# Values of two heads and sums of four heads side by side on TensorE, and the first batch taken in by units

## The chip, the cores and the metric

The kernel runs on one core of one Trainium2 chip. The metric is the device time of one execution in microseconds (us). TensorE (PE in the profile) multiplies matrices into PSUM; VectorE (DVE), ScalarE (ACT) and GpSimd (POOL) work on what lies in SBUF and PSUM; transfers are issued by queues of SyncE (SP), ScalarE and GpSimd. "PEld" is TensorE's loading of the stationary operand of a matmul.

## The reference

Causal attention with a window of 64 positions, followed by a gated two-layer network whose weights are shared by all 4608 tokens.

```python
# q, k, v: (batch 8, heads 8, positions 576, 64) float32
scores = q @ k.T / sqrt(64)                 # per batch and head
mask   = (0 <= row - col) & (row - col < 64)
attn   = softmax(where(mask, scores, -1e9))
x      = (attn @ v) as (8 * 576, 8 * 64)    # heads side by side: 4608 x 512
gate   = maximum(x @ w_gate, 0)             # 512 x 1536
out    = (gate * (x @ w_val)) @ w_out       # 1536 x 512; out is 4608 x 512 float32
```

## The kernel before

The 4608 rows are cut into 24 units of 192 rows (three units to a batch, 8 heads each), and two units make a tile of 384 rows. Attention of a unit gives x turned (features on partitions) in `xt`; the network then runs per tile: `hidden` (groups h of the profile) and `output` (groups op). A small scheduler, the Weaver `W`, places the instructions of the attention units between those of the network: `W.at(t, fn)` queues a piece at a time t of its own clock, and `plan_unit` does so for all the pieces of one unit. Each engine then runs its instructions in the order in which they were written.

In a unit the scores come turned as well: the 128 keys that 64 queries can see lie on partitions. The exponentials `p` are multiplied by a band mask on VectorE (units 0 and 1 add a bias on TensorE before the exponential instead). Values and the sums for the softmax come out of one matmul: each head's value tile holds 64 columns of values and 64 columns of ones.

```python
v16s = [persist.tile([128, UB, H, 128], FP16) ...]     # UB = 3 windows, per head 64 values | 64 ones

def v_load(u):                                          # upper half of each window from memory
    for w in range(UB):
        nc.gpsimd.dma_start(v16s[uu][64:128, w, :, 0:64], v[b, :, k0:k0 + 64] ...)
def v_low(u):                                           # lower half: copy of the window before
    ...                                                 # one or two nc.vector.tensor_copy

def u_pv_wide(u):                                       # units 2 to 23
    d["pv"] = [a_ps.tile([128, 2, 2, 256], FP32, tag="a") for _ in range(2)]
    for c in (0, 2, 1, 3):
        for e in range(2):
            h = 2 * c + e
            for w in range(UB):
                nc.tensor.matmul(d["pv"][c % 2][:, c // 2, e, 64 * w:64 * w + 64],
                                 v16[:, w, 128 * h - 64 * e:128 * h - 64 * e + 128],   # 128 columns
                                 d["p"][h % G][:, h // G, 64 * w:64 * w + 64], ...)

def u_copy(u, n):   # two ScalarE copies for each n in 0, 1: values of even and of odd heads
    ...
def u_sum(u, half): # two VectorE turns for each half: sums of even and of odd heads
    for e in range(2):
        nc.vector.transpose(to[64 * e:64 * e + 64, half::2],
                            d["pv"][half][64 - 64 * e:128 - 64 * e, :, e, 0:U])
def u_back(u):      # reciprocal of one column of each turned block, turned back
    nc.vector.reciprocal(d["rT"], d["sT"]...[:, :, 0:1])
    nc.vector.transpose(d["rs"], d["rT"].to_broadcast([128, nb, 32]))
def u_norm(u):      # xt = values * rs
    nc.vector.tensor_tensor(xt_tile(u // 2)[:, :, c0:c0 + U], d["xs"], rs, MUL)
```

Units 0 and 1 use a narrow form of it, `u_pv`: values of two heads on the two halves of the output's partitions (64 stationary columns each), and then sums from a tile `ones` of 64 columns, in the same way.

q and k of a batch are loaded whole, and turned by VectorE in blocks of 32 (`qk_trans`). The first batch:

```python
for hh in range(2):
    k_first(hh)                    # k in float32 by SyncE's queue, rounded by ScalarE
for hh in range(2):
    qk_load(0, "q", hh)            # q by GpSimd's queue, in float16
...
W.at(7.0, lambda: qk_trans(0, "q", 0)) ; W.at(9.9, lambda: qk_trans(0, "q", 1)) ; ...
W.at(5.3, lambda: u_bias(0)) ; W.at(5.4, lambda: heat(11, ...))   # heat: matmuls of zeros
W.at(6.4, lambda: w_load(*G3[0], 13.7)) ; ...          # nine weight parts of 512 KB
W.at(21.0, lambda: v_ones(2, nc.vector)) ; W.at(21.0, lambda: v_ones(0, nc.vector))
plan_unit(2, 23.0, ...) ; plan_unit(3, 42.15, ...) ; plan_unit(4, 49.3) ; plan_unit(5, 56.95, ...)
T = 67.0                           # then two units to each tile, T += 25.805
...
W.advance(13.7)
ready(1); hidden(0, 0, U, 0, 4, 4)           # first half of tile 0, first third of the features
ready(2); hidden(0, U, TT, 0, 4, 4)          # second half
hidden(0, 0, TT, 4, NF, 4); output_by_rows(0)
ready(3); hidden(1, 0, U); output(1, (0,))
ready(4); hidden(1, U, TT); output(1, (1, 2))
for t in range(2, NU // 2): ...              # whole tiles
```

Of the kernel before, what the change touches and what calls it, by code (L numbers as in the profile page):

```python
# [42 lines left out]
def kernel(  # L43
# [43 lines left out]
    v16s = [persist.tile([128, UB, H, 128], FP16, name=f"v16_{i}") for i in range(UB)]  # L87
# [4 lines left out]
    ident = consts.tile([128, 128], FP16)  # L92

# [21 lines left out]
    def v_ones(i, eng):  # L115
        eng.memset(v16s[i][64 if i == 0 else 0:, 0, :, 64:128], 1.0)
        for w in range(1, UB):
            eng.memset(v16s[i][:, w, :, 64:128], 1.0)  # L118

    def k_zeros():  # L120
        nc.vector.memset(kTs[1][:, :, 0:64], 0.0)

    def constants():
        nc.vector.memset(kTs[0][:, :, 0:64], 0.0)
        nc.vector.memset(v16s[0][0:64, 0], 0.0)
        nc.vector.memset(ones, 1.0)
        nc.vector.memset(ones0, 1.0)
        nc.vector.memset(ones0[0:64], 0.0)

# [40 lines left out]
    def k_first(hh):  # L170

        k32 = nat["k32", hh] = x_sb.tile([128, S // 32 * D], FP32, name="k32", bufs=2)
        nc.sync.dma_start(k32, k[0, G * hh:G * hh + G].rearrange("h (i j) d -> (h i) (j d)", i=32))

    def k_round(hh, part, parts):
        n = S // 32 * D // parts
        if part == 0:
            nat[0, "k", hh] = a_in.tile([128, S // 32 * D], FP16, name=f"k{hh}", bufs=2)
        nc.scalar.copy(nat[0, "k", hh][:, n * part:n * part + n], nat["k32", hh][:, n * part:n * part + n])  # L179
# [8 lines left out]
    def v_load(u):  # L188
        b, uu = divmod(u, UB)
        for w in range(UB):  # L190
            k0 = U * uu + 64 * w
            nc.gpsimd.dma_start(v16s[uu][64:128, w, :, 0:64], v[b, :, k0:k0 + 64].rearrange("h p d -> p h d"))  # L192

    def v_low(u):

        uu = u % UB
        if uu > 0:
            nc.vector.tensor_copy(v16s[uu][0:64, 0, :, 0:64], v16s[uu - 1][64:128, UB - 1, :, 0:64])
        nc.vector.tensor_copy(v16s[uu][0:64, 1:UB, :, 0:64], v16s[uu][64:128, 0:UB - 1, :, 0:64])

    def u_bias(u, gs=range(G)):

        d = units.setdefault(u, {})
        if "st" not in d:
            st_tiles(u)
        d["biased"] = True
        for to in d["st"][0] + d["st"][1] if u == 0 else [d["st"][0][g] for g in gs]:
            n = 1 if u == 0 else 2
            nc.tensor.matmul(to[:, 0:n * U].rearrange("p (n c) -> p n c", c=64), ident,
                             bias[:, None, :].to_broadcast([128, n * UB, 64]),  # L210
                             start=True, stop=False, skip_group_check=True)
# [6 lines left out]
    def st_tiles(u):  # L218
        d = units.setdefault(u, {})
        one = lambda name: f_ps.tile([128, 512], FP32, name=name, tag="h")  # L220
        two = lambda name: a_ps.tile([128, 2, 512], FP32, name=name, tag="a")
        if u == 0:
            d["st"] = [[one("st") for _ in range(G)]]
            halves = [two("st") for _ in range(2)]
            d["st"].append([halves[g // 2][:, g % 2] for g in range(G)])
        elif u == 1:
            half = two("st")
            d["st"] = [[half[:, 0], half[:, 1], one("st"), one("st")]] * 2
        else:
            halves = [two("st") for _ in range(2)]  # L230
            d["st"] = [[halves[g // 2][:, g % 2] for g in range(G)]] * 2
        if u == 0:
            d["spare"] = d["st"][1][3][:, 256:512]
            d["st"] = [[x[:, 0:512 if hh == 1 and g == 3 else 256] for g, x in enumerate(row)] for hh, row in enumerate(d["st"])]

    def u_st(u, hhs=(0, 1)):
        d = units.setdefault(u, {})
        kT, qT = kTs[(u // UB) % 2], qTs[(u // UB) % 2]
        biased = "biased" in d
        if not biased:  # L240
            st_tiles(u)
        ks = U * (u % UB)
        for hh in hhs:
            for w in range(UB):
                c = U * (hh if u else 0) + 64 * w
                for dh in range(2):
                    for g in range(G):
                        rows = slice(32 * g, 32 * g + 32)
                        nc.tensor.matmul(  # L249
                            d["st"][hh][g][:, c:c + 64],  # L250
                            kT[rows, hh, ks + 64 * w:ks + 64 * w + 128, dh],
                            qT[rows, hh, ks + 64 * w:ks + 64 * w + 64, dh],
                            start=(dh == 0 and not biased), stop=(dh == 1),
                            skip_group_check=biased)
        d.setdefault("p", [None] * G)
        return 0.49

    def u_exp(u, g, hh=None):
        d = units[u]
        if not hh:  # L260
            d["p"][g] = a_p.tile([128, 2, U], FP16, name="p")
        if hh is None:
            nc.scalar.activation(d["p"][g].rearrange("p h c -> p (h c)"), d["st"][0][g][:, 0:2 * U], ACT.Exp, scale=scale)  # L263
        else:
            nc.scalar.activation(d["p"][g][:, hh], d["st"][hh][g][:, 0:U], ACT.Exp, scale=scale)
# [6 lines left out]
    def u_pv(u, cs=(0, 2, 1, 3)):  # L272
# [3 lines left out]
        v16 = v16s[u % UB]  # L276
        if u == 0 and cs[0] == 0:
            d["pv"] = [f_ps.tile([128, 2, U], FP32, name="pv", tag="h") for c in cs]
        elif u == 0:
            both = a_ps.tile([128, 2, 512], FP32, name="pv", tag="a")  # L280
            d["pv"] += [both[:, n, 0:2 * U].rearrange("p (s c) -> p s c", s=2) for n in range(2)]
        else:
            halves = [a_ps.tile([128, 2, 512], FP32, name="pv", tag="a") for _ in range(2)]
            d["pv"] = [halves[c % 2][:, c // 2, 0:2 * U].rearrange("p (s c) -> p s c", s=2) for c in range(NC)]
        for c in cs:
            for w in range(UB):
                for e in range(2):
# [3 lines left out]
                        v16[:, w, h, 0:64], d["p"][h % G][:, h // G, 64 * w:64 * w + 64],  # L291
                        start=(w == 0), stop=True, skip_group_check=True)
            for w0, w1, one in ((0, 1, ones0), (1, UB, ones)) if u % UB == 0 else ((0, UB, ones),):
                for e in range(2):
                    h = 2 * c + e
                    nc.tensor.matmul(
                        d["pv"][c][64 * e:64 * e + 64, 1, 64 * w0:64 * w1],
                        one, d["p"][h % G][:, h // G, 64 * w0:64 * w1],
# [3 lines left out]
    def u_pv_wide(u):  # L302

        d = units[u]
        v16 = v16s[u % UB].rearrange("p w h d -> p w (h d)")
        d["pv"] = [a_ps.tile([128, 2, 2, 256], FP32, name="pv", tag="a") for _ in range(2)]
        for c in (0, 2, 1, 3):
            for e in range(2):
                h = 2 * c + e
                for w in range(UB):  # L310
                    nc.tensor.matmul(  # L311
                        d["pv"][c % 2][:, c // 2, e, 64 * w:64 * w + 64],
                        v16[:, w, 128 * h - 64 * e:128 * h - 64 * e + 128],
                        d["p"][h % G][:, h // G, 64 * w:64 * w + 64],
                        start=(e == 0 and w == 0), stop=True,
                        skip_group_check=True)
        return 0.7

    def u_copy(u, n):
# [3 lines left out]
        if u < 2:  # L323
            c = n if u == 0 else (0, 2, 1, 3)[n]
            nc.scalar.copy(d["xs"][:, c], d["pv"][c][:, 0])
        else:
            for e in range(2):
                rows = slice(64 * e, 64 * e + 64)
                nc.scalar.copy(d["xs"][rows, n::2], d["pv"][n][rows, :, e, 0:U])  # L329

    def u_sum(u, half):
        d = units[u]
        if "sT" not in d:
            d["sT"] = a_n.tile([128, NC, U // 32, 32], FP32, name="sT", bufs=1)
        to = d["sT"].rearrange("p g b c -> p g (b c)")
        if u < 2:
            for c in (2 * half, 2 * half + 1) if u == 0 else (half, half + 2):
                nc.vector.transpose(to[:, c], d["pv"][c][:, 1])
        else:
            for e in range(2):  # L340
                nc.vector.transpose(to[64 * e:64 * e + 64, half::2],  # L341
                                    d["pv"][half][64 - 64 * e:128 - 64 * e, :, e, 0:U])

    def u_back(u):
        d = units[u]
        nb = G * (U // 32)
        d["rT"] = a_n.tile([128, nb, 1], FP32, name="rT")
        nc.vector.reciprocal(d["rT"], d["sT"].rearrange("p g b c -> p (g b) c")[:, :, 0:1])  # L348
        d["rs"] = a_n.tile([128, nb, 32], FP32, name="rs", bufs=1)
        nc.vector.transpose(d["rs"], d["rT"].to_broadcast([128, nb, 32]))  # L350
# [14 lines left out]

    def plan_unit(u, T, exp=0.8, mask=1.5, pv=3.9, copy=(4.7, 6.0), norm=(4.8, 6.1, 7.4, 8.7), gap=0.6):

        if u > 5:
            W.at(T - 17, lambda: v_load(u))
        W.at(T + (3.3 if u == 2 else 1.4 if u < 6 else -2.0), lambda: v_low(u))  # L370
        W.at(T, lambda: u_st(u))
        for g in range(G):
            W.at(T + exp + gap * g, lambda g=g: u_exp(u, g))
            if mask is not None:
                W.at(T + mask + gap * g, lambda g=g: u_mask(u, g))
# [250 lines left out]
```

The softmax here doesn't subtract the row's maximum and nothing guards it: scores larger than these inputs give would overflow.

## Time and profile before

The time is 338.88 us, the median of 3 runs (338.54 to 339.09). The profiled execution spans 337.9 us from first to last instruction.

| group in the profile | count | mean of one |
|---|---|---|
| h, 128x384 (line 419), gate and val | 1024 | 326 ns from begin to end |
| op, 128x512 (line 433) | 420 | 379 ns |
| pv, 128x64 (line 311), units 2 to 23 | 528 | 193 ns |
| sT, VectorE's turn of sums, 64x384 (line 341) | 88 | 580 ns |
| xv, ScalarE's copy of values, 64x384 (line 329) | 88 | 473 ns |
| rs, turn back, 128x768 (line 350) | 24 | 978 ns |
| rT, reciprocal, 128x24 (line 348) | 24 | 301 ns |
| p, exponential, 128x384 (line 263) | 92 | 492 ns |
| p, mask, 128x384 (line 270) | 88 | 352 ns |
| qT and kT, turn of a half batch, 128x576 (line 186) | 30 | 1239 ns |

How to read it: matmuls overlap one another in the pipeline, so the time that one adds is the distance from its start to the next one's start, not the mean of one. Groups are named output<-inputs by the program's names, with the line of the kernel. A chain of work goes back from the last instruction to whatever released each step. A row of waits has the waiting group, the group that released it, the total in us, the number of waits and the longest.

### The profile page before, as it was taken

How to read it: one execution, taken by the hardware profiler on the slowest of the kernel's cores; microseconds unless marked ns; L12 is line 12 of the kernel's file. 1: busy time of each engine (PE TensorE's matmuls, PEld its weight loads, DVE VectorE, ACT ScalarE, POOL GpSimd, SP SyncE). 2: the span in 40 equal slices, each digit the busy share in tenths (PEclk: the TensorE clock that was granted, in tenths of full speed). 3: DMA queues.
4: the chain of work that ended last, by engine and by line, in shares of the span. 5: the costliest groups of instructions: out<-in, count | busy, mean ns of one | idle time of the engine just before them, and what ended most of it. 6: DMA issues, size and time to landing. Idle time of an engine off the chain costs nothing.

```text
span 337.9 us, 8605 instructions
## 1 busy us (share of the span) xinstructions
PE 325.5 (96%) x3522; PEld 197.3 (58%) x3522; DVE 260.3 (77%) x493; ACT 176.7 (52%) x383; POOL 74.0 (22%) x121
## 2 busy tenths in 40 slices
PE   8699998999999999999999999999999999999995
PEld 4485485856546656655655655654655664664653
DVE  5878878998998874897989974888889874884430
ACT  4546165745636646645555564564564664653321
POOL 8724341250213221320210410150120200000000
PEclk9989999999999999999999999999999999999999
DMA  8999998496343933491242853296214402001002
GB/s 214 178 206 193 204 203 135 31 139 98 24 77 49 158 51 71 29 185 70 17 53 73 111 75 98 18 143 123 17 10 111 32 3 93 2 2 71 24 0 94
DMA packets 52886, 29.44 MB, mean 87 GB/s; under 512 B 39280, under 2 KB 44272, under 8 KB 52848
## 3 DMA queue, kind: packets, MB, share of 16 engines
q0 software_dynamic: 47088, 18.29, 47.4%
q1 hardware_dynamic: 5616, 10.55, 8.7%
q8 instruction: 27, 0.44, 0.6%
q14 instruction: 11, 0.09, 0.1%
q10 hardware_dynamic: 144, 0.07, 0.1%
HBM read 37.75 MB, written 9.44 MB: 140 GB/s over the span
## 4 chain that ended last, share of the span: by engine, by line
PE 81%; DVE 13%; issue 3%; DMA 2%; ACT 0%; DVEq 0%; ACTq 0%; POOLq 0%
PE h L419 52%; PE op L433 21%; PE pv L311 5%; PE st L249 3%; DVE sT L341 2%; DVE qT L186 2%; DMA q<-in_q_dram 2%; DVE g_sb L407 2%; DVE kT L186 1%; DVE xt L356 1%; DVE rs L350 1%; DVE p L270 1%; PE op L465 1%; DVE v L118 1%; DVE rT L348 0%
## 5 line engine op out<-in xcount | busy, mean ns | idle before, releaser
L419 PE MATMUL h<-xt,wg 128*128 128x384 f16 (+1 forms) x640 | 117.5, 313 | 1.7 <-DVE xt L356 1.7
L419 PE MATMUL h<-xt,wv 128*128 128x384 f16 (+1 forms) x640 | 116.7, 311 | 1.0 <-DVE g_sb L407 1.0
L407 DVE TENSOR_TENSOR g_sb<-r_sb,h 128x384 f16<-128x384 f32 x144 | 78.3, 550 | 48.8 <-PE h L419 47.1
L404 ACT ACTIVATE r_sb<-h 128x384 f32<-128x384 f32 x144 | 70.2, 492 | 67.0 <-PE h L419 55.3
L433 PE MATMUL op<-wo,g_sb 128*128 128x512 f16 x420 | 93.0, 379 | 0.0
L192 POOL DMA_DIRECT2D v<-in_v_dram x72 | 49.5, 696 | 181.0 <-PE pv L311 95.3
L419 PEld LDWEIGHTS <-wg 128*128 128x128 f16 x640 | 61.5, 99 | 36.5 <-DVE xt L356 1.6
L419 PEld LDWEIGHTS <-wv 128*128 128x128 f16 x640 | 59.0, 98 | 31.7 <-issue 1.3
L433 PEld LDWEIGHTS <-g_sb 128*128 128x128 f16 x420 | 40.3, 98 | 46.6
L341 DVE STREAM_TRANSPOSE sT<-pv 64x384 f32<-64x384 f32 x88 | 51.1, 580 | 9.7 <-PE pv L311 7.7
L329 ACT COPY xv<-pv 64x384 f32<-64x384 f32 x88 | 41.6, 473 | 21.5 <-DVE sT L341 8.1
L440 ACT COPY o_sb<-op 128x512 f32<-128x512 f32 x35 | 20.5, 586 | 54.6 <-PE op L433 54.6
L263 ACT ACTIVATE p<-st 128x384 f16<-128x384 f32 x92 | 39.7, 492 | 4.2 <-PE st L249 4.1
L270 DVE TENSOR_TENSOR p<-p,mask 128x384 f16<-128x384 f16 x88 | 27.5, 352 | 0.3 <-ACT p L263 0.2
L350 DVE STREAM_TRANSPOSE rs<-rT 128x768 f32<-128x768 f32 x24 | 23.5, 978 | 0.8
L356 DVE TENSOR_TENSOR xt<-xv,rs 128x768 f16<-128x768 f32 x24 | 22.8, 948 | 0.8
L311 PEld LDWEIGHTS <-v 128*128 128x128 f16 x528 | 18.6, 98 | 4.2 <-issue 0.8
L186 DVE STREAM_TRANSPOSE kT<-k 128x576 f32<-128x576 f32 (+1 forms) x18 | 19.7, 1121 | 1.4 <-ACT k L179 1.3
L311 PE MATMUL pv<-p,v 128*128 128x64 f16 x528 | 19.7, 193 | 1.1 <-DVE p L270 0.6
L186 DVE STREAM_TRANSPOSE qT<-q 128x576 f32<-128x576 f32 x16 | 18.9, 1239 | 1.1 <-DMA q<-in_q_dram 1.1
L249 PEld LDWEIGHTS <-kT 32*128 32x128 f16 x1152 | 11.0, 92 | 10.0 <-issue 9.9
L249 PE MATMUL st<-qT,kT 32*128 32x64 f16 x1152 | 13.9, 189 | 2.3 <-DVE qT L186 2.0
(47 smaller groups left out, 91.8 us busy)
## 6 DMA issues: line engine op xcount, KB each, us to landing
out_dram<-o_sb SPq DMA_DIRECT2D x35, 256.0 KB, 2.0
q<-in_q_dram POOLq DMA_DIRECT2D x16, 288.0 KB, 8.1
v<-in_v_dram POOLq DMA_DIRECT2D x72, 64.0 KB, 3.2
k<-in_k_dram POOLq DMA_DIRECT2D x14, 288.0 KB, 6.1
wg<-in_moe_w_gate_dram POOLq DMA_DIRECT2D x3, 512.0 KB, 10.1
wv<-in_moe_w_val_dram POOLq DMA_DIRECT2D x3, 512.0 KB, 11.9
wo<-in_moe_w_out_dram POOLq DMA_DIRECT2D x3, 512.0 KB, 13.7
k<-in_k_dram SPq DMA_DIRECT2D x2, 576.0 KB, 4.0
```

Of the source, the lines that this page charges most:

```text
L186: nc.vector.transpose(dst.rearrange("p (i j) -> p j i", i=32)[:, j0:j1], src[:, j0:j1])
L192: nc.gpsimd.dma_start(v16s[uu][64:128, w, :, 0:64], v[b, :, k0:k0 + 64].rearrange("h p d -> p h d"))
L249: nc.tensor.matmul(d["st"][hh][g][:, c:c + 64], kT[rows, hh, ks + 64 * w:ks + 64 * w + 128, dh], qT[rows, hh, ks + 64 * w:ks + 64 * w + 64 ...
L263: nc.scalar.activation(d["p"][g].rearrange("p h c -> p (h c)"), d["st"][0][g][:, 0:2 * U], ACT.Exp, scale=scale)
L270: nc.vector.tensor_tensor(p, p, mask[:, None, :].to_broadcast([128, 2 * UB, 64]), MUL)
L311: nc.tensor.matmul(d["pv"][c % 2][:, c // 2, e, 64 * w:64 * w + 64], v16[:, w, 128 * h - 64 * e:128 * h - 64 * e + 128], d["p"][h % G][:, ...
L329: nc.scalar.copy(d["xs"][rows, n::2], d["pv"][n][rows, :, e, 0:U])
L341: nc.vector.transpose(to[64 * e:64 * e + 64, half::2], d["pv"][half][64 - 64 * e:128 - 64 * e, :, e, 0:U])
L404: nc.scalar.activation(part(r_sb), part(h1), ACT.Relu)
L407: nc.vector.tensor_tensor(g_sb[:, f:f + w, c0:c1], part(r_sb), part(h2), MUL)
L419: nc.tensor.matmul(h[:, b * n:b * n + n], wt[:, c, (f + b) * 128:(f + b) * 128 + 128], xt[:, c, c0:c1], start=(c == 0), stop=(c == NC - 1))
L433: nc.tensor.matmul(op, g_sb[:, f, bass.ds(sub * 128, 128)], wo[:, f], start=(f == 0), stop=(f == NF - 1))
```

## The change

For units 2 to 23 the ones leave the value tiles. Values of two heads go side by side: each matmul takes 64 stationary columns and writes half of the output's partitions. The sums come from matmuls with 32 columns of ones: four heads side by side, each on 32 of the output's partitions. This is to halve the streaming of values, to make one VectorE turn and two ScalarE copies per unit enough, and to let a value tile be loaded with fewer transfers. The reciprocals then lie on other partitions than the values that they belong to, and eight small VectorE copies put them in place.

The first batch is loaded by units of 192 rows instead of whole. q and k of its first unit come in float32 by SyncE's and ScalarE's queues; q and k of units 0 to 2 are turned by TensorE (`unit_flip`, a matmul with a permuted identity), and ScalarE and VectorE copy the result to SBUF (`unit_keep`); units 3 to 5 are turned by VectorE, unit by unit. Values are issued behind what is wanted sooner. Unit 2 now has the bias on TensorE instead of the mask on VectorE. In the second tile, `output_by_rows(0)` comes after the first half of `hidden(1)`.

The core of the diff, with cuts marked by "...":

```diff
-    v16s = [persist.tile([128, UB, H, 128], FP16, name=f"v16_{i}") for i in range(UB)]
+    v16s = [persist.tile([128, NG, H, D], FP16, name=f"v16_{i}") for i in range(2)]
...
+    def unit_flip(name, u, hh):
+        if hh == 0:
+            flipped[name, u] = a_ps.tile([128, 2, 512], FP32, name=f"{name}f", tag="a")
+        to = flipped[name, u].rearrange("p a b -> p (a b)")
+        for j in range(J):                                   # J = 6
+            nc.tensor.matmul(to[64 * hh:64 * hh + 64, 128 * j:128 * j + 128],
+                             nat[name, u, hh][:, D * j:D * j + D], turn, ...)
+    def unit_keep(name, u, cc, copy):
+        ...                                                  # half of the heads, PSUM to SBUF
...
     def u_pv_wide(u):
-        d["pv"] = [a_ps.tile([128, 2, 2, 256], FP32, name="pv", tag="a") for _ in range(2)]
-        ...
+        d["pv"] = a_ps.tile([128, 2, 512], FP32, name="pv", tag="a")
+        d["sums"] = a_ps.tile([128, 2, 512], FP32, name="sums", tag="a")[:, 0, 0:2 * U]
+        for r in range(2):
+            for s in range(2):
                 for w in range(UB):
+                    for e in range(2):
+                        h = 2 * (2 * s + r) + e
+                        nc.tensor.matmul(
+                            d["pv"][64 * e:64 * e + 64, r, U * s + 64 * w:U * s + 64 * w + 64],
+                            v16[:, w, h], p_of(u, h)[:, 64 * w:64 * w + 64], ...)
+            for w0, w1, one in ((0, 1, ones0), (1, UB, ones)) if u % UB == 0 else ((0, UB, ones),):
+                for s in range(2):
+                    for e in range(2):
+                        j = 32 * (2 * e + s)
+                        nc.tensor.matmul(
+                            d["sums"][j:j + 32, U * r + 64 * w0:U * r + 64 * w1],
+                            one[:, 0:32], p_of(u, 2 * (2 * s + r) + e)[:, 64 * w0:64 * w1], ...)
...
     def u_sum(u, half=0):
+            nc.vector.transpose(d["sT"].rearrange("p b c -> p (b c)"), d["sums"])
+    def u_recip(u):
+        nc.vector.reciprocal(rH, d["sT"][:, :, 0:1])
+        for e in range(2):
+            for s in range(2):
+                j = 32 * (2 * e + s)
+                for x in range(2):
+                    i = 32 * (2 * e + x)
+                    nc.vector.tensor_copy(d["rT"][i:i + 32, 2 * s:2 * s + 2]..., rH[j:j + 32])
...
         for hh in range(2):
-            k_first(hh)
+            unit_load32("k", 0, hh, nc.sync)
+            unit_load32("q", 0, hh, nc.scalar)
         for hh in range(2):
-            qk_load(0, "q", hh)
+            unit_load32("k", 1, hh, nc.sync)
...
+        heat(8, units[0]["spare"], False)
+        u_pv(0)
+        ...                                  # sums, copies, norm of unit 0
+        for hh in range(2):
+            unit_round("k", 1, hh, pool)
+        w_load(*G3[1], 17.2)
+        v_spread(1, pool)
+        ...                                  # turns, copies by ScalarE, bias, scores, values of unit 1
+        for wt, t in ((V3[1], 23.2), (G3[2], 25.8), (V3[2], 28.4)):
+            w_load(*wt, t)
+        W.at(20.6, lambda: [unit_flip(name, 2, hh) for name in "kq" for hh in range(2)] and None)
+        W.at(20.7, lambda: [unit_keep(name, 2, cc, act) for name in "kq" for cc in range(2)] and None)
+        W.at(21.5, lambda: u_bias(2))
...
-        T = 67.0
+        T = 66.2
...
-            T += 25.805
-        W.advance(13.7)
+            T += 25.505
+        W.advance(12.0)
...
         hidden(0, 0, TT, 4, NF, 4)
-        output_by_rows(0)
         ready(3)
         hidden(1, 0, U)
+        output_by_rows(0)
```

## The prediction

> **What bounds the kernel now.** I read the busy shares on the page first, then the chain of work that ended last, then what TensorE waited for, and last the start times of single groups on TensorE.
>
> ```profile
> PE 325.5 (96%) x3522; PEld 197.3 (58%) x3522; DVE 260.3 (77%) x493; ACT 176.7 (52%) x383; POOL 74.0 (22%) x121
> ...
> PEclk9989999999999999999999999999999999999999
> ```
>
> TensorE is busy 96% of the 337.9 us, at full clock except in one slice. So anything that lasts must take work from TensorE, and the rest can only be waits. The chain in order of time shows where they are:
>
> ```profile
> 1.31 6.16 DMA q<-in_q_dram
> ...
> 17.00 6.93 PE h L419 x64
> ...
> 94.09 7.77 PE op L433 x36
> 101.86 0.65 PE h L419 x4
> 102.51 0.48 PE st L249 x39
> 102.99 4.01 PE h L419 x24
> 107.00 0.70 PE pv L311 x24
> 107.70 7.80 PE h L419 x48
> 115.50 0.48 PE st L249 x39
> 115.98 3.36 PE h L419 x20
> 119.34 0.70 PE pv L311 x24
> 120.04 7.77 PE op L433 x36
> ```
>
> Two stages are to be seen. Up to 17.0 us the chain runs through the load of q, VectorE's turns and the first units. From then on TensorE carries it, and a tile of two units lasts 120.04 - 94.09 = 25.95 us: 15.8 for h, 7.77 for op, 2 x 0.48 for scores, 2 x 0.70 for values with their sums. In a tile without waits a unit's values and sums lie directly on the path. What TensorE waits for after 17 us is little:
>
> ```profile
> PE st L249 <- DVE qT L186: 2.0, 4, 0.6
> PE h L419 <- DVE xt L356: 1.7, 2, 1.2
> ...
> PE h L419 <- DVE g_sb L407: 1.0, 2, 0.7
> ...
> PE pv L311 <- DVE v L199: 0.4, 1, 0.4
> ```
>
> Of these, by the timeline: 0.5 near 31 us (the values wait behind VectorE's fills with ones), 0.3 at 54.3, 1.16 at 58.2, 1.0 from 67 to 69, 0.5 at 92-94, and 0.55 at each of 155 and 234, where the scores of a new batch wait for qT. Together 4.6 us.
>
> The last view is TensorE's timeline around three changes of shape (start, length, group):
>
> ```profile
> 102.18 0.33 PE L419 MATMUL h<-xt,wg 128*128 128x384 f16 x1
> ...
> 102.44 0.55 PE L249 MATMUL st<-qT,kT 32*128 32x64 f16 x48
> 102.92 0.82 PE L419 MATMUL h<-xt,wv 128*128 128x384 f16 x4
> ...
> 11.26 0.50 PE L209 MATMUL st<-bias,ident 128*128 128x384 f16 x2
> 11.69 0.28 PE L289 MATMUL pv<-p,v 128*64 128x64 f16 x6
> 11.80 0.26 PE L296 MATMUL pv<-p,ones 128*64 128x64 f16 x4
> 11.89 0.26 PE L289 MATMUL pv<-p,v 128*64 128x64 f16 x6
> ```
>
> A 384-column h matmul takes 0.163 us from start to start. After the one at 102.18 the scores could begin at 102.34; they begin at 102.44, 0.10 late. Two bias matmuls begun at 11.26 are through by 11.59; the values, of shape 128*64, begin at 11.69, again 0.10 late. By contrast the old wide values (128*128, like h) follow h after 0.16 us, with no loss. So a change of tile shape costs about 0.10 us here, whether rows or columns are cut. Also: six values and four sums of unit 0, done as pairs on the two halves of the columns, take 11.89 - 11.69 = 0.20 us, so the pairs do run at once, at about 29 ns per pair of 64 columns.
>
> [...]
>
> **The change part by part.**
>
> (1) Values and sums, units 2 to 23. Before: 24 matmuls of 64 columns, 24 x 29 ns = 0.70 us, no change of shape. After: 12 pairs x 29 ns = 0.35 us, and two groups of four sums, 192 columns each side by side, 2 x 0.08 = 0.16 us; by columns alone 0.51. But the code goes h, values (128*64), sums (128*32), values, sums, h: five changes of shape. At 0.10 each that is 0.49, so 1.00 us in all. This adds about 0.29 us per unit, 22 x 0.29 = +6.3 us, nearly all on the path. If 64 to 32 columns costs nothing, only the two changes against h remain and a unit takes 0.71, as before. The 4.2 us that the columns alone would save (22 x 0.19) come off only if no change costs anything, which the trace speaks against.
>
> (2) VectorE. Four turns of sums per unit (580 ns each, 2.3 us) become one of 0.58; the reciprocal (301 ns) covers half as much; eight copies of 32 x 12 numbers are added, at an estimated 0.09 each from the smallest VectorE operations (60 to 112 ns): +0.75. Net -1.1 us per unit, off the path except where TensorE waits for VectorE. ScalarE loses two of four 473 ns copies, off the path. I expect the two waits of 0.55 at the new batches to go, since the chain before qT gets shorter by 1.1, and half to three quarters of the 3.0 us between 54 and 94. Against that, units 3 to 5 now need four turns each of 128x192 just before their scores (about 0.53 each, from 0.70 for 288 and 1.24 for 576). Net of all waits: -2.6.
>
> (3) The start. q of unit 0 no longer arrives at 7.49 behind a GpSimd queue: k and q of unit 0 are a third as large (196 KB each) and come by the ScalarE and SyncE queues. k of 576 KB took 4.0 us to land, so I expect all four parts by 4.8. Rounding to 5.7, turns by TensorE to 6.1, two copies on each engine to 6.8, scores to 7.3, four exponentials (0.41 each) to 9.0, values to about 9.6, copies out to 10.2. Then unit 1 goes through ScalarE: four copies of turned k and q (0.45 each) to 12.2, bias and scores to 13, exponentials to 14.6, values to 14.8. TensorE's order puts the first h behind the values of unit 1: about 14.8 against 17.00, while the norm of unit 0 is ready near 12.5 and the first weights near 13. -2.2. The second half of the first tile waits for unit 1's norm, about 3.1 us later at full clock; before it came 4.1 later under the half clock. I count half of that: -0.5.
>
> (4) Unit 2. Its turns now stand in TensorE's line between h matmuls: 24 x 55 ns = 1.3 us, bias 4 x 0.163 = 0.65, changes of shape 0.2; and the bias cannot begin until ScalarE has emptied both buffers (four copies, about 1.1 us more than TensorE has work for). Less 0.15 for scores on 64 rows and less the 0.5 of fills with ones that are gone: +2.6.
>
> Weights: they landed every 2.6 us at about 200 GB/s and TensorE came for them 3 to 5 us late. In the new order the second val part comes at about 23.7 and is wanted at about 27. Hidden.
>
> Sum: 338.9 + 6.3 - 2.6 - 2.7 + 2.6 = 342.5 us.
>
> **The rivals.** (A) 64 to 32 columns costs no change of shape: a unit's values stay at 0.71, so the sum loses its +6.3 and gives about 336. [...] against it: the two kinds of change that the trace has cost the same 0.10. (B) The sums of four heads do not run side by side: 2 x 0.16 more per unit, +3.5 us, about 346. For it: the trace has no 32-column tile; against: 48 score matmuls on four row groups in 0.48 show that four tiles work at once. (C) The start becomes the bound: a wait for POOL's copies of k and v of unit 1, or TensorE at half clock after thin work from 13 to 15, +1 to +3. (D) The waits on VectorE vanish wholly and the start gains 4 us because ScalarE is quicker than counted: -3.
>
> **Range and chances.** I give the five changes at full cost about 0.8, which puts the time at 342.5 give or take 3; the rest, with cheap changes between values and sums, lies near 336 with the same spread. The middle of both is about 341, and 8 in 10 lie between 334.5 and 345.5. Faster by over 2% means below 332.1: rival A and D together. Slower by over 2% means above 345.7: B or C on top of the sum.
>
> **What would show it.** A tile without waits lasts 26.5 us after (25.95, as before, if 64 to 32 columns is free). From a unit's first value to the next h: 0.9 us, with 0.10 lost at each step between values and sums. First h near 14.8. A stall of about 1 us between unit 2's turns and its bias. Turns of sums 22 instead of 88, and no wait of scores for qT at the third and later batches. I am wrong if values and sums together take under 0.7, or if the first h comes after 16.5.

## The result, and the profile after

The time after is 349.43 us (348.79 to 350.78), against 338.99 us before (338.54 to 340.57): a ratio of 1.031, with a 95% interval of 1.026 to 1.035. The change costs 10.4 us where I had expected 2. It lies outside my range. The two profiles are of executions of 350.78 and 339.75 us, so they differ by a little more, 11.2 us of span.

From the page of the changed kernel, the busy shares, and two of its groups (count, busy us, mean ns of one, idle before):

```profile
PE 335.2 (96%) x3746; PEld 197.9 (57%) x3746; DVE 244.3 (70%) x600; ACT 156.9 (45%) x343; POOL 71.5 (20%) x110
...
L399 DVE STREAM_TRANSPOSE sH<-sums 128x384 f32<-128x384 f32 x22 | 12.8, 583 | 16.3 <-PE sums L373 16.3
...
L416 DVE COPY rT<-rH 32x12 f32<-32x12 f32 x176 | 31.3, 178 | 2.9
```

VectorE and ScalarE each lost work (260.3 to 244.3 us and 176.7 to 156.9), and the turns of sums went from 88 to 22, all as meant. TensorE, which sets the end, is busy for 9.7 us more, in a span of 349.1 us instead of 337.9. What VectorE gained is partly spent again on 176 copies of 32x12 numbers, at 178 ns each.

The chain of work over one tile (start us, length us, what):

```profile
153.53 7.88 PE op L506 x36
...
180.35 1.19 PE op L506 x5
```

The tile lasts 180.35 - 153.53 = 26.82 us, against 25.95 before. TensorE's timeline at the end of that tile shows what the four short pieces cost (start, length, group):

```profile
178.53 0.81 PE L492 MATMUL h<-xt,wv 128*128 128x384 f16 x4
179.27 0.38 PE L365 MATMUL pv<-p,v 128*64 128x64 f16 x12
179.58 0.27 PE L373 MATMUL sums<-p,ones 128*32 128x192 f16 x4
179.78 0.38 PE L365 MATMUL pv<-p,v 128*64 128x64 f16 x12
180.08 0.27 PE L373 MATMUL sums<-p,ones 128*32 128x192 f16 x4
180.28 0.39 PE L506 MATMUL op<-wo,g_sb 128*128 128x512 f16 x1
```

The four h matmuls from 178.53 are through at 178.53 + 4 x 0.163 = 179.18; op begins at 180.28. A unit's values and sums cost 1.10 us in place of 0.70. Over the whole trace each of the five changes of shape takes nearly the same: 128 to 64 columns 93 ns, 64 to 32 98, 32 to 64 103, 32 to 128 106. (Each is the time from start to start, less the time after which a matmul of the same shape would have followed: 163 ns for h, 28 for a pair of values, 83 for four sums.) Leaving 64 columns for 32, a change that the trace before did not hold, costs as much as leaving the full array: 98 ns and 93.

What TensorE waited for, by the profile (total us, times, longest):

```profile
PE st L303 <- DVE qT L225: 1.2, 1, 1.2
...
PE h L492 <- ACT o_sb L513: 0.9, 1, 0.9
PE h L492 <- DVE g_sb L480: 0.8, 1, 0.8
```

These stand at 57.8, 67.0 and 40.9 us; with another 0.3 for gates at 77.4 they make 3.2 us, and all others lie in the start. The waits at the third and later batches are gone. The 0.9 is new: an output buffer is asked for while its last contents are still on the way out, a transfer that began at 59.31 and took 6.96 us.

The beginning of the chain, and then one microsecond of the same kernel (stretch, length, TensorE busy with its groups, granted clock, DMA share, GB/s):

```profile
1.50 5.61 DMA q<-in_q_dram
...
10.92 1.01 PE st L267 x8
...
19.18 0.78 PE h L492 x8
```

```profile
11.00:12.00 1.00, 1.00 (x14) 0.50 1.17 185
```

q of unit 0 lands at 7.1, hardly sooner than before (7.47), for all that a third as much is loaded. At 10.92 eight matmuls of zeros ("st", line 267) run before unit 0's values, and TensorE has half its clock from 10.9 to 14.3. The first h, which by the timeline begins at 19.11, was at 17.00 before.

**Where the 10.4 us are.** Between the two profiles the start of the last op group moves by 345.31 - 334.00 = 11.3 us. The last h of the first tile moves by 39.70 - 36.13 = 3.6 us, the values of unit 2 within it; 21 further units cost 0.406 us each more, 8.5 us; TensorE's waits after 36 us fall from 4.1 to 3.2, -0.9. These make 11.2 us.

### The profile page after: what moved, and what is told of

It reads as the page before. It is cut to its first block, busy times and chain, and to the rows that moved or that the text cites. A ratio compares the mean times of both kernels' runs of the same rounds, so it can differ in the third digit from the quotient of the medians. Undisturbed runs are those within 1.5% of the kernel's fastest.

```text
span 349.1 us, 9055 instructions
## 1 busy us (share of the span) xinstructions
PE 335.2 (96%) x3746; PEld 197.9 (57%) x3746; DVE 244.3 (70%) x600; ACT 156.9 (45%) x343; POOL 71.5 (20%) x110
## 3 DMA queue, kind: packets, MB, share of 16 engines
q0 software_dynamic: 52912, 18.31, 46.3%
## 4 chain that ended last, share of the span: by engine, by line
PE 87%; DVE 4%; DMA 4%; ACT 3%; issue 1%; ACTq 0%; DVEq 0%
PE h L492 52%; PE op L506 23%; PE pv L365 4%; PE st L303 3%; PE sums L373 2%; DMA out_dram<-o_sb 2%; DMA q<-in_q_dram 2%; DVE rT L416 1%; ACT p L313 1%; DVE g_sb L480 1%; PE op L538 1%; DVE qT L232 1%; DVE xt L428 1%; ACT kA L217 0%; PE st L260 0%
## 5 line engine op out<-in xcount | busy, mean ns | idle before, releaser
L238 POOL DMA_DIRECT2D v<-in_v_dram x32 | 28.7, 898 | 129.8 <-PE sums L373 90.9
L313 ACT ACTIVATE p<-st 128x384 f16<-128x384 f32 x96 | 41.7, 492 | 10.0 <-PE st L303 8.2
L416 DVE COPY rT<-rH 32x12 f32<-32x12 f32 x176 | 31.3, 178 | 2.9
L387 ACT COPY xv<-pv 128x384 f32<-128x384 f32 x44 | 20.0, 482 | 29.1 <-PE pv L365 29.1
L399 DVE STREAM_TRANSPOSE sH<-sums 128x384 f32<-128x384 f32 x22 | 12.8, 583 | 16.3 <-PE sums L373 16.3
L365 PEld LDWEIGHTS <-v 128*64 128x64 f16 x528 | 11.8, 111 | 9.1 <-issue 5.0
L365 PE MATMUL pv<-p,v 128*64 128x64 f16 x528 | 16.8, 200 | 0.0
L232 DVE STREAM_TRANSPOSE kT<-k 128x576 f32<-128x576 f32 x12 | 14.6, 1232 | 0.1
L232 DVE STREAM_TRANSPOSE qT<-q 128x576 f32<-128x576 f32 x12 | 14.1, 1242 | 0.0
L303 PEld LDWEIGHTS <-kT 32*128 32x128 f16 x1008 | 9.6, 92 | 8.0 <-issue 7.2
```

The lines of the kernel that those rows point to most:

```text
L232: nc.vector.transpose(dst.rearrange("p (i j) -> p j i", i=32)[:, j0:j1], src[:, j0:j1])
L238: nc.gpsimd.dma_start(v16s[b % 2][:, g], v[b, :, 64 * g - 64:64 * g + 64].rearrange("h p d -> p h d"))
L365: nc.tensor.matmul(d["pv"][64 * e:64 * e + 64, r, U * s + 64 * w:U * s + 64 * w + 64], v16[:, w, h], p_of(u, h)[:, 64 * w:64 * w + 64], st ...
L416: nc.vector.tensor_copy(d["rT"][i:i + 32, 2 * s:2 * s + 2].rearrange("p g b c -> p (g b) c"), rH[j:j + 32])
```

## The experiments

My theory after seeing this: five changes of shape per unit at 0.10 us each, plus slightly dearer pairs, make over two thirds of the loss, and a start that became later makes the rest. Its rivals: the sums themselves are slow, and not the changes; the start or the waits on VectorE carry most of it. Each run had the kernel before beside it on the same chip.

### The new values and sums alone, in the kernel before

```diff
-                         d["pv"][c % 2][:, c // 2, e, 64 * w:64 * w + 64],
-                         v16[:, w, 128 * h - 64 * e:128 * h - 64 * e + 128], ...
+                         d["pv"][64 * e:64 * e + 64, r, U * s + 64 * w:...], v16[:, w, h, 0:64], ...
+            ...          d["sums"][j:j + 32, ...], one[:, 0:32], p_of(u, ...)
```

The copies, the one turn of sums and the eight small copies come with it. The loads, the first batch and the fills with ones, which nothing reads any more, stay as before.

> The kernel before with only the new values and sums from unit 2 on (values in pairs, sums in fours, eight small copies); the fills with ones are kept though nothing reads them. Theory D (five changes of tile shape per unit at 0.10 us each): a unit's values and sums go from 0.70 to 1.11 us on TensorE, 22 x 0.41 = +9.1, some waits on VectorE fall away (up to -1.5), so 346.5 to 348. Rival S (the new start is the main loss): the change to values and sums costs at most 3 us, so at most 342.

346.35 us beside 339.08, ratio 1.021 (1.019 to 1.023): +7.3 us. The first h is at 17.21 (17.00 before), and a unit costs 1.10 us as in the full change. 22 x 0.406 is 8.9; part of it is given back by shorter waits. The values and sums alone carry about 70% of the loss.

### All sums of a unit behind all its values: three changes instead of five

```diff
+        for r in range(2):
             for w0, w1, one in ((0, 1, ones0), (1, UB, ones)) if u % UB == 0 else ((0, UB, ones),):
```

> The kernel after, with both groups of sums behind all values of a unit: three changes of shape instead of five. Theory D: 2 x 0.10 + 0.02 less per unit, 22 x 0.22 = 4.9 us less, about 344.5. Rival B (what costs is the 32-column sums themselves, not the changes between): no difference, 349 to 350.

345.38 us, ratio 1.018 (1.017 to 1.020): about 4.1 us less than the change. TensorE's timeline of this run:

```profile
175.66 0.81 PE L493 MATMUL h<-xt,wv 128*128 128x384 f16 x4
176.41 0.57 PE L365 MATMUL pv<-p,v 128*64 128x64 f16 x24
...
177.19 1.04 PE L507 MATMUL op<-wo,g_sb 128*128 128x512 f16 x4
```

Those are the same matmuls in another order. They take 177.19 - (175.66 + 0.65) = 0.88 us in place of 1.10; 22 such differences are 4.8 us. So it is the changes and not the sums. (That TensorE goes back and forth between two outputs in PSUM is not it either: the next run does the same without a gap, six pairs and the step to the sums in 0.22 us.)

### Sums from 64 columns of ones: two changes

```diff
-                            d["sums"][j:j + 32, U * r + 64 * w0:U * r + 64 * w1],
-                            one[:, 0:32], p_of(u, 2 * (2 * s + r) + e)[:, 64 * w0:64 * w1], ...
+                            d["sums"][64 * e:64 * e + 64, r, U * s + 64 * w0:U * s + 64 * w1],
+                            one, p_of(u, 2 * (2 * s + r) + e)[:, 64 * w0:64 * w1], ...
```

Sums now stand on the partitions of their values, in two VectorE turns per unit, and the eight small copies fall away.

> The kernel after, with the sums from 64 columns of ones, two heads side by side: values and sums have one shape, so two changes of shape are left, while the sums stream twice as long. Two VectorE turns of sums instead of one, no small copies. Theory D: 0.40 values + 0.33 sums + 0.20 changes = 0.93 us per unit instead of 1.11, 22 x 0.18 = 4 us less, about 345.5, and up to 1 less where TensorE waited for VectorE. Rival B: more columns streamed, 22 x 0.17 = 3.7 more, about 353.

343.26 us (342.16 to 346.5), ratio 1.014 (1.009 to 1.019): about 6 us less than the change.

```profile
173.45 0.81 PE L483 MATMUL h<-xt,wv 128*128 128x384 f16 x4
174.19 0.38 PE L365 MATMUL pv<-p,v 128*64 128x64 f16 x12
174.41 0.34 PE L372 MATMUL sums<-p,ones 128*64 128x192 f16 x4
...
175.03 0.82 PE L497 MATMUL op<-wo,g_sb 128*128 128x512 f16 x3
```

The sums stream twice as much and the unit is still shorter: 175.03 - 174.10 = 0.93 us. From values to sums nothing is lost any more: six pairs of values take 174.41 - 174.19 = 0.22 us. This explains 22 x 0.18 = 4 us. The other 2 go with the waits: after 30 us TensorE no longer waits for VectorE at all, only 1.4 us once for an output buffer. Still, 0.93 is more than the old 0.70.

### One small matmul per unit, in the kernel before

A single matmul of 32 columns and 64 positions amid each unit's values, whose output nothing reads.

```diff
+            if c == 2:
+                nc.tensor.matmul(d["pv"][0][0:32, 0, 0, U:U + 64], ones[:, 0:32], d["p"][0][:, 0, 0:64], ...)
```

> The kernel before with one matmul more per unit, 32 columns of ones on 64 columns of one head, written to a part of PSUM that nothing reads, in the middle of the values. Theory D: its work is about 0.03 us, but it brings two changes of shape, 2 x 0.10, so 0.22 to 0.23 per unit and 22 x 0.225 = 5 us more, about 344. If a change of shape were cheap and the 32-column sums or the pairs were the cost: 22 x 0.03 = 0.6 more, within the noise of before.

344.11 us beside 339.51, ratio 1.015 (1.013 to 1.016): +4.6 us.

```profile
106.59 0.51 PE L311 MATMUL pv<-p,v 128*128 128x64 f16 x12
107.03 0.20 PE L318 MATMUL pv<-p,ones 128*32 128x64 f16 x1
...
107.53 0.65 PE L422 MATMUL h<-xt,wv 128*128 128x384 f16 x3
```

The 24 values and the small matmul take 107.53 - 106.59 = 0.94 us instead of 0.70. 64 columns streamed once cost 0.03 us (0.70 / 24); the way in and out of the other shape is the rest. This has neither the change's loads nor its VectorE work, and shows the cost of a change by itself.

The same trace tells what the half clock costs at the start of the kernel before. Up to unit 2's values the two programs are the same, but this execution had its full clock throughout (a mean of 1.00), and the profile of before has half of it from 16.7 to 20.1 us. The second third of the features begins, in the profile of before and in this one:

```profile
23.76 2.76 PE L419 MATMUL h<-xt,wg 128*128 128x384 f16 x16
...
23.02 2.76 PE L422 MATMUL h<-xt,wg 128*128 128x384 f16 x16
```

Of the 0.74 us, 0.14 were there at the first h (17.00 and 16.86), so the half clock costs about 0.6 there.

### The old values in the changed kernel

From unit 2 on the values come with the ones again, filled by VectorE; everything else as in the change, but for planned times that leave room for them.

```diff
-        d["pv"] = a_ps.tile([128, 2, 512], FP32, name="pv", tag="a")
+        d["pv"] = [a_ps.tile([128, 2, 2, 256], FP32, name="pv", tag="a") for _ in range(2)]
...
+            W.at(t, lambda i=i, w0=w0: v_ones(i, w0))      # six times, by nc.vector
```

> The kernel after, with the values and sums of the kernel before (one matmul of 64 value and 64 ones columns) from unit 2 on; the first batch by units and everything else stays. Theory D: 22 x 0.41 = 9.1 less, about 340.3, plus or minus 1 for waits on VectorE and for the fills with ones; what is left over the kernel before is the start's share, about 1.5 to 3. Rival S: still above 345.

354.4 us, ratio 1.043 (1.038 to 1.047): a miss by 14 us. The first of TensorE's waits:

```profile
PE op L498 <- DVE g_sb L472: 3.4, 2, 2.6
```

This is the largest; waits of the scores for qT (3.2 us) and of h for gates (2.4) follow, all of them on VectorE. I had put the fills and the four turns of sums back on a VectorE that the new order had already filled with the turns of units 3 to 5. Part of the 14 us is clock: the trace has half of it from 78.9 to 85.7 us, and the four executions took 351.6 us at a mean granted clock of 1.00 and 354.0 to 355.1 at 0.984 to 0.990. The run shows that the new order needs the lighter VectorE; it does not isolate the start. A later run (below) was to do that.

### The start: without the matmuls of zeros

```diff
             u_exp(0, c)
-        heat(8, units[0]["spare"], False)
         u_pv(0)
```

> The kernel after without the eight matmuls of zeros between unit 0's exponentials and its values. Theory H: they write a bank that the last exponential reads, so they wait for it and hold the values back by about 1.0 us; without them the values of unit 0 follow the exponentials, the first h comes 1.0 to 1.6 us earlier (19.1 to about 17.8) and 1 to 1.5 us come off, about 348. Rival T: they keep the clock up; without them half clock lasts longer, and the first h stays near 19.

348.98 us, ratio 1.027 (1.024 to 1.030), an interval that overlaps that of the change (1.026 to 1.035). The first h comes at 17.88 instead of 19.11, 1.2 us sooner, and the profiled span is 1.1 shorter (348.0 to 349.1). But unit 0's scores began 0.4 sooner in this profile, before any matmul of zeros was missed, so their part is about 0.8. The run with all sums last has the start of the change, and its q was rounded at 6.67, as here (6.71); its first h is at 18.31, and against that the gain is 0.4. Unit 0's values now waited 0.89 us for VectorE's copy of v, which had landed late. The half clock came all the same, at 11.4 to 14.8, and lasted 3.4 us as it did with them (10.9 to 14.3), so nothing speaks for rival T. So these matmuls did delay the values, by less than their own length.

### The start: k of unit 1 kept from the first loads

```diff
-        for hh in range(2):
-            unit_load32("k", 1, hh, nc.sync)
...
-        for hh in range(2):
-            unit_load("q", 1, hh)
+        for name in "kq":
+            for hh in range(2):
+                unit_load(name, 1, hh)
```

k of unit 1 now goes by GpSimd's queue in float16, and GpSimd's two rounding copies fall away.

> The kernel after with k of unit 1 by GpSimd's queue in float16 behind the values of unit 0, instead of float32 by SyncE's queue. Theory K: the second half of q of unit 0 lands at 7.1 because it shares the transfer engines with k of unit 1; it lands near 5.3 now, the scores of unit 0 begin near 7.3 instead of 8.9, the first h comes up to 1.5 earlier. Rival V: the small packets of the values hold it, and it lands at 6.8 or later as before.

349.75 us, ratio 1.030 (1.028 to 1.032): no gain. The second half of q of unit 0 is rounded from 6.27 instead of 7.13, that of k from 5.85 instead of 4.65, and the first h is at 17.37 instead of 19.11; the last op is 1.7 us sooner in the profile, but the measured time did not follow. The two profiles are not of like executions: that of the change is of its slowest one, 350.78 us at a mean granted clock of 0.995, while its other three took 348.79 to 349.57 at 0.998, and this run's four took 349.36 to 349.91 at 0.998 to 1.000. At like clocks nothing is left of the 1.7 us. The weights are now issued behind two more loads, and h waits 0.45 us for a val part. How early q and k arrive depends on what loads beside them, but the weights set the next limit. In this profile TensorE has its full clock at the start (1.00 from 6 to 22 us), so its first h is earlier for that reason too. From the end of unit 0's exponentials to the first h it took 7.3 us, against 8.2 in the profile of the change and 7.9 in the runs with all sums last and with 64 columns of ones, which have its start and the half clock; so by estimate the half clock makes 0.6 to 0.9 of it, if the other order of loads plays no part there.

### All of it together

64 columns of ones, no matmuls of zeros, k of unit 1 later, and six output buffers (`bufs=6` for `o_sb`).

> The kernel after with the sums from 64 columns of ones (two changes of shape), without the eight matmuls of zeros, with k of unit 1 by GpSimd's queue, and with six output buffers instead of three. If the causes add: 343.3 - 1.2 - 1.5 - 1.4 (TensorE's wait for an output buffer) = about 339. If the start's parts hide behind one another (the first weights, unit 1's copies on ScalarE), about 342.

341.58 us beside 339.4, ratio 1.006 (1.004 to 1.009). Of the 10.4 us lost, 8 are back, and TensorE waits for nothing after 30 us. It is still slower than before: a unit's values and sums are 0.23 us longer, about 5 us in all (the 4.1 us of waits that are gone pay for most of that), and the first h is at 18.2, where the values of unit 0 waited 1.8 us for the copy of v.

### The new start with the old values

The three repairs of the start and the buffers, values and ones as in the kernel before, fills by GpSimd instead of VectorE, and the old plan of times.

> The new start as in the run before, but values and sums as in the kernel before from unit 2 on, the ones filled in by GpSimd, and the planned times of the kernel before. Theory D: 0.70 instead of 0.93 us per unit, 22 x 0.23 = 5 us less than the run with all fixes, about 334 to 336. If VectorE cannot carry four turns of sums together with the four turns of q and k of units 3 to 5, TensorE waits for it between 35 and 95 us and the time is 338 to 343.

342.94 us, ratio 1.010 (1.008 to 1.012). The middle of the run is the kernel before to the hundredth: from the last h of the sixth tile to that of the eleventh it takes 130.44 us, before 130.45. The loss is there at the end of the first tile, whose last h is at 38.13 instead of 36.13. TensorE's timeline where the first val groups begin:

```profile
19.47 1.50 PE L484 MATMUL h<-xt,wv 128*128 128x192 f16 x16 [0.83 <-DMA wv<-in_moe_w_val_dram]
```

The first h is at 17.14, only 0.14 later than before and at full clock (1.00 from 6 to 22 us), but TensorE then waits for the val weights, and unit 2's turns, bias and the wait for ScalarE follow. So the new start is no gain even without these faults, and the half clock is not what kept it from one. At equal clock the loss is larger: in the run with one small matmul, which begins as the kernel before does, the last h of the first tile is at 35.39, 0.24 us of it for that matmul, so 3.0 us are lost by then. The measured loss is 3.5.

### Unit 2's turns earlier

```diff
-        W.at(20.6, lambda: [unit_flip(name, 2, hh) ...])
+        W.at(17.2, lambda: [unit_flip(name, 2, hh) ...])     # its copies move with it
```

> The run with the fixed start and the old values, with unit 2's turns of q and k on TensorE placed before the second third of the features instead of just ahead of the bias, so that ScalarE's four copies run beside h. If TensorE's two waits at the bias (0.61 and 0.28) are the cost of that order, 0.9 us less: span 339.7 instead of 340.6, about 342. If q and k of unit 2 have not landed by 23.4 us, TensorE waits for them instead and nothing is gained.

343.66 us, ratio 1.012 (1.010 to 1.014): nothing gained.

```profile
25.05 0.52 PE L212 MATMUL qf<-turn,qu 128*64 128x128 f16 x6 [1.05 <-DMA qu<-in_q_dram]
```

The wait on ScalarE is exchanged for a wait of 0.21 + 1.05 us on loads.

### Can the order alone improve the kernel before?

Two variants of the kernel before, with its values. In the first GpSimd fills the ones, the turns of each batch are planned 1.5 us earlier, and unit 4's norm is moved; in the second VectorE keeps the fills, at other times, and half of the turns go 9 us earlier still.

```diff
-        W.at(21.0, lambda: v_ones(2, nc.vector))
-        W.at(21.0, lambda: v_ones(0, nc.vector))
+        W.at(12.25, lambda: v_ones(2, nc.gpsimd))
+        W.at(13.2, lambda: v_ones(0, nc.gpsimd))
...
-        early, late = (-7.4, -6.0, -4.6, -3.2), (-20.3, -18.9, -17.5, -16.1)
+        early, late = (-8.9, -7.5, -6.1, -4.7), (-20.3, -18.9, -17.5, -16.1)
```

> The kernel before, values and sums as they were; fills with ones by GpSimd, the turns of q and k at a new batch planned 1.5 us earlier, the first turn of batch 2 behind the norm of unit 3, the norm of unit 4 later. If the waits on VectorE that the profile of before shows can be moved away by order alone: 0.5 near 31 us, 1.16 at 58, part of 1.0 at 67, twice 0.55 at 155 and 234, so 2 to 3.5 less, 336 to 337. If VectorE is full there, the waits only move: 338.5 to 340.

> The kernel before with the order changed once more: fills with ones stay on VectorE but where it has gaps, k of a new batch is turned 9 us earlier than before and q where it was planned 1.4 us earlier, the first turn of batch 2 behind the norm of unit 3, the norm of unit 4 only a little later. If order alone can take the waits away: 1.5 to 3 us less than before, 336 to 337.5. If VectorE is full between 50 and 95 us: the waits move, 338 to 339.5.

340.45 us, ratio 1.002 (1.000 to 1.004), and 341.4 us, ratio 1.005 (1.003 to 1.007). The first is no gain: waits moved to other places, and the first h slipped from 17.00 to 18.40. Of these 1.40 us 0.40 were lost sooner (unit 0's second scores begin at 11.37 instead of 10.97); for the rest see the timeline of VectorE and GpSimd in that run:

```profile
14.33 1.27 DVE L198 COPY v<-v 64x512 f16<-64x512 f16 x1
14.41 1.05 POOL L118 MEMSET v<- 128x512 f16 x2
```

The copy of v that unit 1's values need takes 1.27 us while GpSimd fills; its mean in the kernel before is 0.29. The next copy of v, twice as wide and begun at 15.53, when the fills were over, took 0.41, against a mean of 0.43 before. That the fill held the first one up is my inference from these two; no run here took the fill away from beside that one copy, so it is not shown.

No version that I ran is faster than the kernel before.

## Why the prediction was wrong

I compare step by step with the sum 342.5, before I weighed it with rival A. In the profiles the change cost 11.2 us where that sum had +3.6. The error of 7.6 us has three parts that were too low and a small one that was too high.

**(3) The start, the step that failed: 3.9 us.** I had "First h near 14.8" and called myself wrong after 16.5. It came at 19.11, 2.1 us later than before instead of 2.2 sooner. Term by term, of these 4.3 us:
- "I expect all four parts by 4.8": the last landed at 7.1, +2.3. I had scaled the old landing time by the size and had not counted what loads beside it; with k of unit 1 moved away q was rounded 0.9 us sooner, though k of unit 0 came later. What else held it is not shown.
- From landing to the end of unit 0's exponentials I had 4.2 us; it took 3.8, -0.4.
- Unit 0's values: I had 0.6 us. The eight matmuls of zeros before them, which I had not counted at all, took 1.0, and the values at half clock 1.2: +1.7. Rival C had named the half clock for 13 to 15 us; it stayed out of the sum.
- From there to the first h I had 5.2 us; it took 6.0, +0.8.

The second half of the tile gained 0.9, where I had 0.5. All this is one execution. The runs with all sums last and with 64 columns of ones have the same program up to unit 2: in them q was rounded from 6.67 and 6.91 instead of 7.13, and the first h came at 18.31 and 18.57. So up to 0.8 us of the 4.3 can be chance, and the error of the step is 3.1 to 3.9 us; that it failed, and by these terms, stands in all three.

**(1) Values and sums: 2.4 us, the size of a term.** The mechanism held: five changes of shape, each about 0.10, rival A refuted, rival B too (four sums do run side by side, 3 ns from one start to the next). The size was off: "1.00 us in all" measured 1.10 us. Pairs take 32 ns and not 29, the first pair after a change 49 to 52, the sums 0.19 instead of 0.16, the changes 0.50 instead of 0.49. My own lines spoke against 29: six values and four sums of unit 0 hold the columns of six pairs, and 0.20 us for six is 33 each. The addition was 0.41 and not 0.29 per unit, and it lay on the path in all 22.

**(2) VectorE: 1.7 us, again a size.** I had the waits cut by 2.6 us, and they fell by 0.9. The net of "-1.1 us per unit" rested on small copies "at an estimated 0.09 each", from the smallest operations of the trace; they take 178 ns. Eight cost 1.42 instead of 0.75, and the net is about -0.4. The waits at later batches went as said, but between 40 and 78 us others stayed or came, one of them for an output buffer, which no part of my working looked at. With the copies gone, in the run with 64 columns of ones, the waits on VectorE after 30 us vanish, as the step wanted.

**(4) Unit 2: right, 0.6 us too high.** From the first h of the second third to the last h of the tile took 14.71 us against 12.37, +2.3 with unit 2's values, where I had +2.6 and +0.3. The stall of "about 1 us" between turns and bias measured 0.9.

"Weights: Hidden" held in the changed kernel only because its start was late; with the first h near 17 TensorE waits for a val part (0.45 and 0.83 us in two runs). An earlier start would have met it, so 14.8 would probably not have paid in full; no run came near it.

The top of my range, 345.5, is the sum and 3 us; three errors in the same direction made 8. Rival B's figure was wrong in itself: 2 x 0.16 more per unit is 22 x 0.32 = 7.0 us and not 3.5, which would have come to 349.5, next to the measured time, by luck and for a cause that the runs exclude. (The half clock of the kernel before, which (3) reckons with, lay at 16.7 to 20.1 us.) Rival A, at a chance of one fifth, moved the middle down by 1.5 us although the trace held two kinds of change with the same cost and none that was free.

Two halves nearly add up to the whole: new values alone +7.3 us, new start with old values (three faults removed) +3.5, the whole +10.4. The second is not the start of the change as it stands, so that they fit so well is in part luck.

What stays open: what held q of unit 0 until 6.7 to 7.1 us; and what decides when the half clock comes, which was at 10.9 us in the profile of the change, at 11.4 without the matmuls of zeros, at 11.5 with all repairs together, and not at all between 6 and 22 us in the profiles with k of unit 1 later alone and with the new start and old values.

## What to carry to other kernels

Count changes of tile shape before columns saved: here each cost about 0.10 us, which is as much as three pairs of 64-column matmuls, so by this reckoning narrow tiles can pay only in long runs of one shape, and no run here had one long enough; put everything of one shape together (0.88 us a unit instead of 1.10 here). Time small cross-partition copies by the number of instructions and not by their size (178 ns for 12 numbers a partition, against 290 for 512 in float16). A start is a race among loads (q of unit 0 was rounded at 6.27 us with k of unit 1 out of the way, at 6.67 to 7.13 beside it): before moving a first consumer forward, list what shares the loads with it, and what the consumer after it waits for. Before two profiles are compared, look at the mean granted clock of both executions: here one of 0.995 beside one of 0.998 made a gain that the times did not have.

## What the runs showed of the hardware

- A change of shape costs 93 to 106 ns from start to start wherever it was worked out: among 128, 64 and 32 columns, and from 128 to 32 rows (258 - 163 = 95).
- The first pair of 64-column matmuls after a change takes 49 to 52 ns, those after it 32. Four sums of 32 columns and 192 positions take 0.09 us together.
- Half of the granted clock for 3.4 us cost the start of the kernel before about 0.6 us (one pair of executions).
- A VectorE copy of 64x512 float16 took 1.27 us beside GpSimd's fills and has a mean of 0.29 in the kernel before. In the changed kernel a bias operation of 128x64 took 0.96 us from 2.36 while GpSimd filled (2.26 to 3.28), 0.17 in the kernel before. That the fills were the cause is not shown.
